# Attention and Fourier mixing on one core: slots in twos, an earlier copy of the mask's factors, and work moved from TensorE and GpSimd to VectorE

## The chip, the cores and the metric

The kernel runs on one core of one Trainium2 chip. The metric is the time of one execution in microseconds (us) on the device. Executions of one kernel lie within 0.1 to 0.7% of each other here. A difference of 2% is the threshold for calling a change faster or slower.

## The reference

Four batches of block-sparse attention (8 heads, 768 positions, head size 64) are joined into x of 768 x 512. Each x then goes through a Fourier mixing with a normalised two-layer channel product.

```python
scores = scale * np.matmul(q, k.transpose(0, 1, 3, 2))      # (4, 8, 768, 768)
scores = np.where(mask, scores, -1e9)                       # window, global and random blocks of 32
attn = np.exp(scores - max); attn = attn / attn.sum(-1)
x = np.matmul(attn, v)                                      # joined to (4, 768, 512)
u = x + np.real(np.fft.fft2(x))                             # along seq and d_model
un = (u - mean(u)) / np.sqrt(var(u) + 1e-6)
out = u + np.maximum(un @ w_ch1, 0.0) @ w_ch2
```

## The kernel before

The heads go in 16 pairs, four pairs per batch. A pair's weights are made in 12 units of 128 keys by 384 queries, and two units are one **slot**, so there are 96 slots, 24 per batch. From the second batch on, the mixing of the batch before (folds on VectorE, Fourier products `zp` on TensorE, then channel products `xp`, `yp`, `z`, `y`) is put between the slots. The order of all instructions is fixed when the kernel is built: a small model of the engines (`when`, `busy`) decides what fits where.

A slot computes the scores s of its two units, then adds o of the two units of the slot before:

```python
def slot(sl):
    phase, r = divmod(sl, SB)          # SB = 24 slots per batch
    n, s = divmod(sl, SP)              # pair, slot of the pair
    units = range(SLOT * sl, SLOT * sl + SLOT)
    if sl < B * SB:
        for u, ps in scores(units):    # PE: s <- qT,kT, and s <- factors for the mask
            weigh(u, ps)               # ACT: exponential; then sums of the weights
    ...
    if 0 < sl <= B * SB:
        done = [u - SLOT for u in units]
        for u in done:
            values(u)                  # PE: o <- e,vr
    ...
    for at, a, half in ((1, 0, 0), (2 if n > 0 else 3, 0, 1), (4, 1, 0), (5, 1, 1)):
        if s == at and n + 1 < BY_VECTOR:                       # BY_VECTOR = 2 * NP + 1 = 9
            short.append(("t", 0.0, lambda a=a, half=half: turn(n + 1, a, half)))   # on PE
    ...
    if BY_VECTOR <= n + 1 < len(pairs):                         # on VectorE
        for at, fn, args in ((0, squares, (n + 1, 0)), (1, flip_blocks, (n + 1, 0)),
                             (2, in_order, (n + 1,)), (4, flip_blocks, (n + 1, 1)),
                             (5, squares, (n + 1, 1))): ...
    w_steps(sl)                        # VectorE rounds a chunk of the channel weights
    if sl == SB - 3:
        keep_factors()
```

Where TensorE adds the mask itself (the first batch, and the second until its channel products begin), it multiplies two small factors into the scores. These factors first lie in the two buffers that the second batch needs for its sums of weights, so they are copied away near the end of the first batch, into a buffer that a weight chunk used before:

```python
at_k = acc_p.tile([P, 2, 2 * HS], BF16, tag="acc", name="at_k")   # acc_p has two buffers
at_q = acc_p.tile([P, 2, 2 * HS], BF16, tag="acc", name="at_q")
factors = {"at": (of_k, off_q)}
def keep_factors():
    kept = room(2, [P, 2, S], "factors", BF16)
    for a, t in enumerate(factors["at"]):
        nc.sync.dma_start(out=kept[:, a, :], in_=t)
    factors["at"] = kept[:, 0, :], kept[:, 1, :]                   # used from the next slot on
```

From the second batch on, the sum of the weights over the keys is gathered by GpSimd, two adds of 384 columns per unit (`acc<-acc,e`), and `total` sums it over the partitions on TensorE (`sp<-acc,pick`).

## Time and profile before

| | before |
|---|---|
| time, median of the 4 runs beside the changed kernel | 1088.8 us (1086.9 to 1092.2) |
| span of the profiled run | 1090.0 us |
| start of slot 20, 24, 48, 72 (from the trace) | 104.5, 129.0, 296.1, 559.2 us |
| TensorE's waits, slots 20 to 24 / slot 24 to the end | 3.7 / 15.4 us |

"TensorE's waits" are all the holes between the end of one matmul record and the start of the next, added up over the trace. The span is divided at the starts of slots, because a slot is the same piece of the attention in every version; how much of the mixing lies ahead of it can differ. From the page of the kernel before, the shares of the chain that ended last, and the group of GpSimd's adds (line, engine, operation, output and inputs, shape, count; then busy us and mean ns; then the idle time ahead and what ended it):

```profile
PE 88%; DVE 6%; ACT 2%; issue 1%; DMA 1%; SPq 1%; POOL 0%; DVEq 0%; ACTq 0%; POOLq 0%
...
L602 POOL TENSOR_TENSOR acc<-acc,e 128x384 f32<-128x384 f32 x192 | 200.4, 1077 | 128.4 <-DVE e L590 118.8
```

The chain is TensorE's for 88%, and VectorE, ScalarE and transfers come in only where TensorE waits. GpSimd's 200 us of adds are on the chain for 0%, so moving some of them away can help only by what waits behind them.

### The profile page before, as it was taken

The page shows a single profiled execution, that of the slowest core. Times are in us where ns is not written, and L with a number is a line of the kernel's source. Part 1 is how long each engine was busy: PE and PEld are TensorE (multiplying, and loading weights), DVE is VectorE, ACT ScalarE, POOL GpSimd, SP SyncE. Part 2 cuts the span into 40 slices and gives each one's busy share as a digit, 9 for nine tenths or more (in the row PEclk, how much of TensorE's full clock was granted, in tenths as well). Part 3 has the DMA queues.
Part 4 walks back from the last instruction along what each step waited for, and adds up shares of the span by engine and source line. Part 5 has one row for each costly group of instructions (what it writes and reads, how often), then busy time and mean ns, then how long its engine had stood idle before and what let it go on. Part 6 is the DMA issues. An engine that isn't in the chain of part 4 may idle for free.

```text
span 1090.0 us, 12509 instructions
## 1 busy us (share of the span) xinstructions
PE 1056.0 (97%) x4410; PEld 538.6 (49%) x4410; DVE 648.6 (60%) x1203; ACT 378.8 (35%) x762; POOL 274.2 (25%) x302
## 2 busy tenths in 40 slices
PE   8999879999999999999999999999999999999996
PEld 4333335454444555443444555443344555568575
DVE  5899682664468255665577446555556355575663
ACT  5988644552331212343342302334230202220210
POOL 1000084852243001355455000344630001000000
PEclk9999899999999999999999999999999999999998
DMA  7757311110010001223211000212000001000001
GB/s 223 229 164 240 94 30 30 39 35 15 15 29 1 1 0 31 57 39 55 44 21 32 1 0 15 63 33 39 13 8 7 1 0 30 29 1 0 1 19 44
DMA packets 108483, 47.07 MB, mean 43 GB/s; under 512 B 95854, under 2 KB 101244, under 8 KB 108412
## 3 DMA queue, kind: packets, MB, share of 16 engines
q1 hardware_dynamic: 106524, 45.38, 16.4%
q10 hardware_dynamic: 1856, 0.79, 0.3%
q8 instruction: 37, 0.61, 0.2%
q14 instruction: 34, 0.28, 0.1%
q0 software_dynamic: 32, 0.01, 0.0%
HBM read 37.11 MB, written 6.29 MB: 40 GB/s over the span
## 4 chain that ended last, share of the span: by engine, by line
PE 88%; DVE 6%; ACT 2%; issue 1%; DMA 1%; SPq 1%; POOL 0%; DVEq 0%; ACTq 0%; POOLq 0%
PE y L1066 23%; PE z L1010 15%; PE s L565 11%; PE o L615 10%; PE yp L1010 8%; PE yy L1129 6%; PE xp L1010 4%; PE zp L823 2%; PE tp L498 1%; PE sp L681 1%; PE s L575 1%; PE utp L935 1%; PE zp L794 1%; SPq L653 1%; PE sp L695 1%
## 5 line engine op out<-in xcount | busy, mean ns | idle before, releaser
L602 POOL TENSOR_TENSOR acc<-acc,e 128x384 f32<-128x384 f32 x192 | 200.4, 1077 | 128.4 <-DVE e L590 118.8
L565 PE MATMUL s<-qT,kT 64*128 64x384 f32 x768 | 154.4, 517 | 5.3 <-DVE e L590 3.8
L615 PE MATMUL o<-e,vr 128*64 128x384 f32 x768 | 148.7, 509 | 0.0
L1069 DVE TENSOR_TENSOR x<-y,x 128x512 f32<-128x512 f32 x72 | 49.7, 691 | 147.8 <-PE y L1066 147.8
L1066 PE MATMUL y<-w_sb,hA 128*128 128x512 f32 x288 | 131.1, 598 | 1.7 <-ACT zs L825 1.7
L1066 PE MATMUL y<-w_sb,hB 128*128 128x512 f32 x288 | 129.0, 597 | 0.7 <-DVE x L1069 0.7
L590 DVE TENSOR_TENSOR e<-s,mask 128x768 f32<-128x768 f32 x106 | 96.3, 949 | 46.6 <-ACT s L588 44.9
L588 ACT ACTIVATE s<-s 128x768 f32<-128x768 f32 x106 | 80.3, 789 | 118.2 <-PE s L565 117.6
L602 POOL TENSOR_TENSOR acc<-e 128x384 f32<-128x384 f32 x48 | 49.9, 1061 | 237.6 <-ACT e L585 129.1
L565 PEld LDWEIGHTS s<-qT,kT 64*128 64x128 f32 x768 | 63.7, 186 | 80.4 <-issue 23.0
L1010 PE MATMUL z<-unT,t 128*128 128x384 f32 x256 | 93.0, 486 | 0.0
L1015 DVE TENSOR_TENSOR hA<-z,hA 128x384 f32<-128x384 f32 x64 | 35.7, 558 | 89.5 <-PE z L1010 88.7
L1066 PEld LDWEIGHTS y<-w_sb,hB 128*128 128x128 f32 x288 | 53.2, 190 | 67.6 <-issue 65.8
L615 PEld LDWEIGHTS o<-e,vr 128*64 128x64 f32 x768 | 47.4, 138 | 76.3 <-issue 72.3
L1066 PEld LDWEIGHTS y<-w_sb,hA 128*128 128x128 f32 x288 | 52.4, 190 | 65.7 <-issue 58.5
L886 POOL TENSOR_SCALAR st<-st 128x1 f32<-128x1 f32 x24 | 6.7, 280 | 280.6 <-DVE st L885 280.2
L585 ACT ACTIVATE e<-s 128x768 f32<-128x768 f32 x86 | 65.0, 812 | 28.0 <-PE s L575 26.6
L1019 ACT ACTIVATE hA<-hA 128x384 f32<-128x384 f32 x64 | 33.5, 523 | 117.8 <-DVE hA L1015 117.4
L1010 PEld LDWEIGHTS z<-unT,t 128*128 128x128 f32 x256 | 48.6, 190 | 33.9
L1019 ACT ACTIVATE hB<-hB 128x384 f32<-128x384 f32 x64 | 33.5, 523 | 86.5 <-DVE hB L1015 86.5
L1010 PE MATMUL xp<-unT,w_sb 128*128 128x384 f32 x128 | 47.7, 495 | 0.3 <-DVE x L1069 0.3
L1010 PE MATMUL yp<-unT,w_sb 128*128 128x384 f32 x128 | 46.9, 489 | 0.5 <-DVE un L859 0.5
(202 smaller groups left out, 1389.7 us busy)
## 6 DMA issues: line engine op xcount, KB each, us to landing
wraw<-in_moe_w_ch_dram SPq DMA_DIRECT2D x32, 512.0 KB
vr<-in_v_dram SPq DMA_DIRECT2D x30, 192.0 KB
qr<-in_q_dram SPq DMA_DIRECT2D x48, 64.0 KB
x<-oT SPq DMA_DIRECT2D x192, 12.0 KB
kr<-in_k_dram SPq DMA_DIRECT2D x14, 192.0 KB
qb<-in_q_dram SPq DMA_DIRECT2D x28, 96.0 KB
kb<-in_k_dram SPq DMA_DIRECT2D x28, 96.0 KB
out_dram<-x SPq DMA_DIRECT2D x16, 128.0 KB
```

What stands on the lines that cost most here:

```text
L565: nc.tensor.matmul(s[:, i, 0:HS], kT[rows, c * P:(c + 1) * P], qT[rows, queries], start=True, stop=u not in by_pe)
L585: nc.scalar.activation(out=e, in_=s[:, :, 0:HS], func=ACT.Exp, scale=scale)
L588: nc.scalar.activation(out=s[:, :, 0:HS], in_=s[:, :, 0:HS], func=ACT.Exp, scale=scale)
L590: nc.vector.tensor_tensor(out=e, in0=s[:, :, 0:HS], in1=m.broadcast_to([P, 2, HS]), op=ALU.mult)
L602: nc.gpsimd.tensor_add(out=acc, in0=e_of[u - 1][:, i, :] if c == 1 else acc, in1=e[:, i, :])
L615: nc.tensor.matmul(o[D * i:D * i + D, :], vt[:, i, c, :], e[:, i, :], start=(c == 0), stop=(c == C - 1))
L1010: nc.tensor.matmul(to, a[:, k, :], c[:, k, :], start=(k == 0), stop=(k == ND // 2 - 1))
L1015: tt(out=to, in0=ps, in1=a, op=ALU.add)
L1019: nc.scalar.activation(out=h, in_=h, func=ACT.Relu)
L1066: nc.tensor.matmul(y, hs[0, half][:, l, m * P:(m + 1) * P], w2_sb[:, 4 * r + l, :], start=(l == 0), stop=(l == 3))
L1069: nc.vector.tensor_tensor(out=x[:, m, :], in0=y, in1=x[:, m, :], op=ALU.add)
L1129: nc.tensor.matmul(ps, a[:, k, :], c[k // 2][:, k % 2, :] if isinstance(c, list) else c[:, k, :], start=(k == 0), stop=(k == 3))
```

## The change

In the main the change does five things. It runs slots in twos from the first channel products on, about 250 us into the run (s, o, o, s in place of s, o, s, o), so that TensorE changes its tiling mode less often. It gives VectorE some of the second batch's adds (one of 768 columns in place of two of 384). It turns q and k of pairs 5 to 8 on VectorE. It puts measured durations into the model. And it copies the mask's factors two slots earlier. (It also moves the start of the mixing, some loads and one bank of transposes, in lines not shown.) Its core, with cuts:

```diff
-    BY_VECTOR = 2 * NP + 1
+    BY_VECTOR = NP + 1
 ...
+    def gather(u):
+        ...
+        if u in by_pe and factors["at"] and max(when["DVE"], at) + 1.0 < max(when["POOL"], at) + 2.9:
+            nc.vector.tensor_tensor(out=acc, in0=start, in1=e, op=ALU.add)
+            acc_at[n, half] = busy("DVE", 1.0, at) + HOP
+        else:
+            for i in range(2):
+                nc.gpsimd.tensor_add(out=acc[:, i, :], in0=start[:, i, :], in1=e[:, i, :])
+            acc_at[n, half] = busy("POOL", 2.9, at) + HOP
 ...
+        OPS = {fold_0: 1, fold_1: 1, fold_e: 3, fold_2: 2}     # folds: longer beside GpSimd
 ...
+        opens = sl % 2 == 0
+        state["paired"] |= opens and len(late) > 0
+        paired = state["paired"]
 ...
+        if paired and len(due) == 2 and due[0] % SP % T == T - 1:
+            sum_up()
+        got = scores(units) if sl < B * SB else ()
+        if paired and len(due) == 2:
+            sum_up()
+        for u, ps in got:
+            weigh(u, ps)
 ...
-        if sl == SB - 3:
+        if sl == SB - 5:
             keep_factors()
```

More of the change, by code (lines that the diff above doesn't have):

```diff
@@ L481, with turn_on @@
     turned, e_of, acc_of, o_of, sums_of, x_of, sp_of = {}, {}, {}, {}, {}, {}, {}
-    s_at, e_at, oT_at, acc_at = {}, {}, {}, {}
+    s_at, e_at, e_free, oT_at, acc_at = {}, {}, {}, {}, {}
+    def turn_on(n, a, half):
+        return "m" if n > NP and (a, half) == (0, 1) else "t"
     def turn(n, a, half):
         t = loaded[n, a]
-        if half == 0:
+        first_of = (n, a) not in turned
+        if first_of:
             turned[n, a] = tp_p.tile([P, S], FP32, tag="qk"[a] + "T", name="qk"[a] + "T")
@@ L490, in turn @@
         first = n == 0 and half == 0
-        tag, pool = ("m", ps_m) if first and a == 0 else ("t", ps_t)
+        tag, pool = ("m", ps_m) if first and a == 0 or turn_on(n, a, half) == "m" else ("t", ps_t)
         tp, at = pool.tile([P, 512], FP32, tag=tag, name="tp"), bank(tag)
@@ L510, in turn @@
             give(at, end)
-        if half == 1:
+        if not first_of:
             flat = t.rearrange("p t r i d -> p (t r i d)" if a == 0 else "p c i d -> p (c i d)")
@@ L585, in weigh @@
             nc.scalar.activation(out=e, in_=s[:, :, 0:HS], func=ACT.Exp, scale=scale)
-            e_at[u] = busy("ACT", 0.8, s_at[u]) + HOP
+            e_at[u] = busy("ACT", 0.8, max(s_at[u], e_free.pop(u - 2 * SLOT, 0.0))) + HOP
         else:
@@ L592, in weigh @@
             e_at[u] = busy("DVE", 0.97, busy("ACT", 0.8, s_at[u]) + HOP) + HOP
-        if n < NP:
+            if n >= NP:
+                gather(u)
+    def gather(u):
+        n, w = divmod(u, UP)
+        half, c = divmod(w, C)
+        if c == 0:
             return
-        if c > 0:
-            acc_at[n, half] = busy("POOL", 2.0, e_at[u]) + HOP
         if c == 1:
             acc_of[n, half] = acc_p.tile([P, 2, HS], FP32, tag="acc", name="acc")
-        for i in range(2 if c > 0 else 0):
-            acc = acc_of[n, half][:, i, :]
-            nc.gpsimd.tensor_add(out=acc, in0=e_of[u - 1][:, i, :] if c == 1 else acc,
-                                 in1=e[:, i, :])
+        acc, e = acc_of[n, half], e_of[u]
+        start = e_of[u - 1] if c == 1 else acc
+        at = max(e_at[u], acc_at.get((n, half), 0.0))
+        if u in by_pe and factors["at"] and max(when["DVE"], at) + 1.0 < max(when["POOL"], at) + 2.9:
[5 more added lines that the diff above has]
+            acc_at[n, half] = busy("POOL", 2.9, at) + HOP
+        e_free[u] = acc_at[n, half]
     def values(u):
@@ L616, in values @@
                              start=(c == 0), stop=(c == C - 1))
+        if u in by_pe and n >= NP:
+            gather(u)
         if c == C - 1:
@@ L901, in d @@
         def d(us, fn, *args):
-            return "d", lambda: fn(*args), 0.0, 0.0, us
+            return "d" + "d" * OPS.get(fn, 0), lambda: fn(*args), 0.0, 0.0, us
+        OPS = {fold_0: 1, fold_1: 1, fold_e: 3, fold_2: 2}
         first = [d(1.8, fold_0, 0), d(1.8, fold_0, 1), d(1.0, fold_1, 0), d(0.9, fold_e),
@@ L1207, with behind @@
     W_PACE = 1.42
-    short, apart, late = deque(), deque(), deque()
-    state = {"w": 0, "got": 0, "owed": 0.0, "ready": 0.0}
+    short, apart, late, due = deque(), deque(), deque(), deque()
+    asked = set()
+    needed = set()
+    state = {"paired": False, "total": None, "w": 0, "got": 0, "owed": 0.0, "ready": 0.0}
     def channel_step():
         late.popleft()[0]()
+    def behind(kind):
+        at = max(when["DVE"], state["ready"])
+        return 0.75 * (len(kind) - 1) if when["POOL"] > at else 0.0
     def do_apart():
         kind, fn, pe, act, dve, _ = apart.popleft()
-        if kind in "dw":
+        if kind[0] in "dw":
+            dve += behind(kind)
             state["ready"] = busy("DVE", dve, rstd_at[0] if kind == "w" else state["ready"]) + HOP
@@ L1241, in gap @@
                 break
-            if kind in "dw":
+            if kind[0] in "dw":
+                dve += behind(kind)
                 if kind == "w" and rstd_at[0] > max(when["DVE"], when["PE"]) + 0.2:
@@ L1281, in begin, with rest, once @@
         apart.append(("-", go, 0.0, 0.0, 0.0, hold))
+    def rest():
+        return state["owed"] if late and state["owed"] >= late[0][1] / 2 else 0.0
+    def once(*of):
+        if of in asked:
+            return False
+        asked.add(of)
+        return True
     def w_loads():
@@ L1296, in slot, with sum_up @@
         units = range(SLOT * sl, SLOT * sl + SLOT)
-        if sl < B * SB:
-            for u, ps in scores(units):
-                weigh(u, ps)
-        if not late:
-            gap(1.5)
-        if 0 < sl <= B * SB:
-            done = [u - SLOT for u in units]
+        opens = sl % 2 == 0
+        state["paired"] |= opens and len(late) > 0
+        paired = state["paired"]
+        def sum_up():
+            at = due.popleft()
+            done = range(SLOT * at, SLOT * at + SLOT)
             for u in done:
                 values(u)
-            if phase == 0 or sl == SB:
+            if at < SB:
                 add_up(done)
@@ L1309, in slot @@
                 e_of.pop(u)
-        if s == 3 and n + 2 < len(pairs):
+        if paired and len(due) == 2 and due[0] % SP % T == T - 1:
[5 more added lines that the diff above has]
+            weigh(u, ps)
+        if not paired and not late:
+            gap(1.5)
+        while due and (opens or not paired):
+            sum_up()
+        due.append(sl)
+        if s >= (4 if paired else 3) and n + 2 < len(pairs) and (n + 2, 0) not in loaded:
             load_q(n + 2)
@@ L1315, in slot @@
         reuse = n % NP == 0 and phase >= 2
-        if sl > 0 and s == (5 if reuse else 3) and sl <= B * SB:
+        if s >= (5 if reuse else 3) and (n, 0) in oT_at and once(n):
             b, j = pairs[n]
@@ L1339, in slot @@
             short.append(("t", acc_at[n - 1, 1], lambda: total(n - 1)))
+            state["total"] = short[-1]
+        if r == 0:
+            needed.clear()
+            needed.update(map(id, short))
         if n + 1 < len(pairs):
-            for at, a, half in ((1, 0, 0), (2 if n > 0 else 3, 0, 1), (4, 1, 0), (5, 1, 1)):
-                if s == at and n + 1 < BY_VECTOR:
-                    short.append(("t", 0.0, lambda a=a, half=half: turn(n + 1, a, half)))
+            for at, a, half in ((1, 0, 0), (2 if n > 0 else 3, 0, 1),
+                                (3 if paired else 4, 1, 0), (5, 1, 1)):
+                if s >= at and n + 1 < BY_VECTOR and once(n + 1, a, half):
+                    short.append((turn_on(n + 1, a, half), 0.0,
+                                  lambda a=a, half=half: turn(n + 1, a, half)))
             if s == 1:
@@ L1351, in slot @@
             short.append(("m", 0.0, lambda: mask_step(sl - 4)))
-        if r == 1 and 0 < phase:
+        if r > 0 and 0 < phase and not needed.intersection(map(id, short)) and once("mixing", phase):
             begin(phase - 1)
@@ L1357, in slot @@
         state["owed"] = min(state["owed"], pace) + pace if late else 0.0
-        gap(max(state["owed"], 0.0))
-        while late and state["owed"] >= late[0][1] / 2:
+        more = paired and opens and sl < B * SB
+        if not more:
+            gap(rest())
+        while not more and rest():
             state["owed"] -= late[0][1]
             channel_step()
-            gap(max(state["owed"], 0.0))
-        while short and (s in (2, 5) or len(short) > 1 or phase == 0 or r == 0):
+            gap(rest())
+        must = (3, 5) if paired else (2, 5)
+        soon = r == 0 and all(i[1] < when["PE"] + 1.0 for i in short)
+        if s == 1 and state["total"] in short:
+            short.remove(state["total"])
+            state["total"][2]()
+        while short and (not more or soon) and (
+                s in must or len(short) > 1 or phase == 0 or soon or sl == B * SB):
             ready = [i for i in short if max(i[1], min(free[i[0]])) <= when["PE"] + 0.1]
-            if not ready and s not in (2, 5) and r > 0 and sl > 1:
+            if not ready and s not in must and 1 < sl < B * SB and not soon:
                 break
```

## The prediction

> **What bounds the kernel now.** I read the page's busy table and its slices first.
>
> ```profile
> PE 1056.0 (97%) x4410; PEld 538.6 (49%) x4410; DVE 648.6 (60%) x1203; ACT 378.8 (35%) x762; POOL 274.2 (25%) x302
> PE   8999879999999999999999999999999999999996
> POOL 1000084852243001355455000344630001000000
> PEclk9999899999999999999999999999999999999998
> ```
>
> TensorE is the bound: 97% busy, and a busy span can be lengthened only by more matmul time or a stall. So I ask two things: what matmul time the change takes away, and which stalls (the slices with 8 or less; the clock dips in slice 4, and in the windows of 25 us at 100 to 125 and 150 to 175, 0.86 each) it removes or makes. For the first I read TensorE's timeline, start to start, where the third batch's slots lie between channel products:
>
> ```profile
> 316.43 3.70 PE L1066 MATMUL y<-w_sb,hA 128*128 128x512 f32 x8
> 320.06 1.56 PE L565 MATMUL s<-qT,kT 64*128 64x384 f32 x8
> 321.55 1.51 PE L615 MATMUL o<-e,vr 128*64 128x384 f32 x8
> 322.99 3.70 PE L1066 MATMUL y<-w_sb,hA 128*128 128x512 f32 x8
> ```
>
> A slot is s (1.49 us) and o (1.44 us). Eight records of either cost 4 x 0.316 = 1.26 us in steady state (the starts of successive pairs inside a group lie 0.316 apart). The y group takes 3.63 us here, 3.44 us where another full-array group is on both sides. So each change between full array, two row tiles (s) and two column tiles (o) costs 0.15 to 0.2 us, three per slot: about 0.55 us.
>
> For the stalls I list TensorE's waits along the same timeline:
>
> ```profile
> 113.40 1.62 PE L565 MATMUL s<-qT,kT 64*128 64x384 f32 x8 [0.36 <-ACT e L585]
> 118.39 0.82 PE L575 MATMUL s<-factors 64*128 64x384 bf16 x4 [3.37 <-DMA factors<-at_q]
> 119.15 0.90 PE L637 MATMUL xt<-ident,oT 128*128 128x128 f32 x3
> 119.98 2.83 PE L615 MATMUL o<-e,vr 128*64 128x384 f32 x8
> ...
> 142.78 0.44 PE L498 MATMUL tp<-ident,qr 128*128 128x128 f32 x2 [1.12 <-ACT qT L507]
> ...
> 159.93 1.56 PE L794 MATMUL zp<-cs_sb,sa 128*128 128x385 f32 x4 [3.64 <-DVE sa L767]
> 162.19 1.01 PE L795 MATMUL zp<-cs_sb,e 128*128 128x192 f32 x2 [0.71 <-DVE e L767]
> ...
> 465.68 1.78 PE L565 MATMUL s<-qT,kT 64*128 64x384 f32 x8 [1.73 <-DVE e L590]
> ```
>
> After each long wait the same o group takes 2.83 us instead of 1.51 us: the clock has halved, and that costs another 2 to 3 us.
>
> **What the Trainium skill says.** "TensorEngine Tiling (Array Packing)", Key Properties: changing the tiling mode, not just the tile, drains TensorE. The 0.15 to 0.2 us per change agrees. "TensorE: Matmul & The Clock Gate", Part 1: after an idle window of about 3.4 us the clock falls to half until a busy window has passed. The waits of 3.37 and 3.64 us followed by double durations agree. "SBUF — State Buffer", Who interferes with whom: a VectorE instruction with two SBUF inputs and a GpSimd instruction that reads SBUF shut each other out for their whole length. Here the scaling of x (L723) takes 0.68 us alone and 1.48 us beside GpSimd's adds, which grow from 1.00 to 1.44 us: agrees.
>
> **The change, part by part.** I used the order of instructions of both programs; TensorE's, VectorE's and ScalarE's are the same up to the 20th slot (of 96).
>
> 1. *Transposes of q and k of pairs 5 to 8 go to VectorE.* 48 transposes fewer at 0.109 us: -5.2 us of TensorE. The two places where a pair's second q transpose waited for the one bank (1.12 us at 142.78 and 212.33) go too: -2.2 us. VectorE gets 4 x (0.96 + 1.52) us; ScalarE gets four reorderings of six copies, 2 x (0.43 + 0.31 + 0.19) = 1.9 us each.
> 2. *Slots in twos, s o o s instead of s o twice.* Going through both TensorE orders group by group, with each other tile shape counted as its own mode, I count 337 changes of mode before and 293 after: 44 x 0.19 = -8.4 us. Valuing every group by the shortest time that its kind took between the same neighbours gives the same sum for parts 1 to 3 within 2 us.
> 3. *The mask is added by TensorE for 4 slots longer in the second batch* (the mixing of the first batch is released later): 16 bf16 matmuls at 0.08 us and their mode changes, +1.7 us.
> 4. *VectorE adds up 23 of the second batch's units, 768 wide,* about 0.9 us each. GpSimd loses 46 adds of 1.0 to 1.5 us. Neither is TensorE's time, but GpSimd's adds were interleaved with the folds that the first Fourier product waits for (159.93). That product now also stands some two slots later. The wait (3.64 + 0.71) and the slow clock after it (about 3 us: o 2.83 for 1.51, the second zp group 2.20 for 1.4, the rest smaller) should go: -7.5 us.
> 5. *The copy of the mask's factors is issued in slot 19 instead of 21, and first used in slot 20 instead of 22.* This looks like a gain of 6 us. I do not believe it. The copy writes a buffer that the 27th weight chunk used, and in both programs it waits for the same VectorE instruction, that chunk's last rounding. The timelines of VectorE and of the DMA queue:
>
> ```profile
> 109.79 0.69 DVE L461 TENSOR_TENSOR w_sb<-w_sb,wraw 128x512 f32<-128x512 f32 x1
> ```
> ```profile
> 110.39 3.82 SPq L252 DMA_DIRECT2D qr<-in_q_dram  x6
> 114.31 0.55 SPq L478 DMA_DIRECT2D factors<-at_k  x1
> 114.91 0.60 SPq L478 DMA_DIRECT2D factors<-at_q  x1
> ```
>
> That rounding ends at 110.5. Before, the copy then stood behind six loads of q, went at 114.31 and released TensorE at 118.39, 4.1 us later. After, it can go at 110.5 and release at about 114 (3.3 to 4.1 us). But slot 20 wants it where it now does its mask matmuls, at 105.92. So TensorE waits about 8 us instead of 3.4, and pays the slow clock as before: +4.5 us.
>
> 6. *New waits in the second batch.* There a slot is now s 1.39, mask 0.42, o 1.44 = 3.26 us, with less else between. ScalarE needs 2 x 0.8 us for its exponentials, and their PSUM banks are wanted again about 2 us after the mask matmuls end. So some 0.5 us is left per slot; a reordering of 1.9 us or one that waits for a VectorE still folding uses it up. Four times about 1 us, plus squares and adds that hold the four weight buffers, plus the end of the stage, where VectorE has adds, a turn and the differences in a row: +6 us, an estimate, the least certain term.
> 7. *Batches three and four.* Runs of slots without channel work wait for weights (1.73 us at 465.68 and again at 720.17; 0.2 us in single slots). In twos, two o groups lie between some s groups, so part of this goes: -3 us.
>
> Sum: -5.2 - 2.2 - 8.4 + 1.7 - 7.5 + 4.5 + 6 - 3 = -14.1 us. 1087.5 - 14.1 = 1073.4, so **1073 us**, 1.3% less. The end (after the last attention slot TensorE's order is the same) contributes nothing.
>
> **Rivals.**
> - *The factor copy is in time.* For: it no longer stands behind the q loads, and that is plainly why it was moved. Against: the rounding's end at 110.5. If it were in time, parts 5 and the old loss change from +4.5 to -6: about 1063 us, faster by over 2%.
> - *VectorE becomes the bound of the second batch.* It is busy 59 of the 102 us from 129 to 231; adds (21 us) and turns (10 us) are added to a stage that also gets shorter. For: 90 us of work in some 95 us, in strict order, with TensorE's weights waiting on adds behind folds. Against: part of today's 59 us is waiting for GpSimd, which shrinks, and the last part of the stage's work is the channel stage's. If it binds, +10 us more: about 1083.
> - *The mode changes are hidden or the pairs starve on PSUM.* Between s and the next s there must be exponential and mask product of two units, about 2.7 us; the doubled o gives 2.7 us, a single o at a half's end only 1.44. If each of some 24 pairs waited 0.3 us, 7 us of part 2 is given back: about 1080.
>
> **Range and chances.** The certain part (1, 2, 3) is about -14 us; the stalls (4 to 7) are near zero in sum, each several us uncertain. All favourable gives 1060, all unfavourable 1085. 8 in 10: 1061 to 1084. Faster by 2% means below 1065.7, which needs the factor copy in time or nearly no new waits: 0.22. Slower by 2% would take a new bound through three batches: 0.01.
>
> **What would show it right or wrong.** Part 5: a wait of about 8 us at the first matmul with factors, near 114 us, DMA named, and slow groups after it; right if over 6, wrong if under 2. Part 4: no wait over 1 us at the first zp group. Part 2: o in groups of 16 records at about 2.7 us, s of the second slot without a wait. Part 1: no tp group after 130 us. Part 6: waits of s for ScalarE's e between 130 and 230, in sum 4 to 8 us. TensorE's busy time should fall by 10 to 14 us, plus or minus what the slow clock changes. The prediction is wrong if TensorE's stalls, counted from its timeline, do not come to about the 22 us of today less some 5.

## The result, and the profile after

The changed kernel is correct. Its median is **1080.86 us** (1080.1 to 1081.2, 4 runs), that of the kernel before 1088.81 us beside it. Ratios in this text are the mean time of one kernel's runs over that of the other's of the same rounds, so not quite the ratio of the medians. Here it is 0.9923, with a 95% interval of 0.9895 to 0.9950: about 0.8% less, within 2%.

The page of the changed kernel, where the prediction showed that of before (busy time, then TensorE's slices in tenths of busy time, then GpSimd's):

```profile
PE 1042.1 (97%) x4378; PEld 537.1 (50%) x4378; DVE 661.5 (61%) x1226; ACT 376.4 (35%) x742; POOL 227.4 (21%) x256
...
PE   8999789999999999999999999999999999999996
POOL 1000062323600001265454000354630001000000
```

TensorE's busy time fell by 13.9 us, but the span only by 10.5 (1090.0 to 1079.5). The fifth slice is worse, 7 for 8. TensorE's timeline there (start, length, engine, line, operation, and in brackets the idle time ahead of it and its releaser), with the last instruction of the weight chunk on VectorE and the copy in the DMA queue:

```profile
104.92 1.56 PE L570 MATMUL s<-qT,kT 64*128 64x384 f32 x8
115.64 0.82 PE L580 MATMUL s<-factors 64*128 64x384 bf16 x4 [9.16 <-DMA factors<-at_q]
116.39 2.83 PE L633 MATMUL o<-e,vr 128*64 128x384 f32 x8
```
```profile
110.17 0.69 DVE L462 TENSOR_TENSOR w_sb<-w_sb,wraw 128x512 f32<-128x512 f32 x1
```
```profile
110.92 0.53 SPq L479 DMA_DIRECT2D factors<-at_k  x1
111.50 0.60 SPq L479 DMA_DIRECT2D factors<-at_q  x1
```

TensorE arrives at slot 20's mask product at 106.5 and stands for 9.16 us: the copy goes out at 110.92, just after the rounding ends at 110.86, and releases TensorE at 115.64. The o group after it takes 2.83 us where others take 1.51: the trace grants TensorE half its clock from 110.92 to 121.16.

The first Fourier product, which had waited 3.64 us, waits no more. Eleven microseconds ahead of it there is a new wait. TensorE's timeline, then VectorE's:

```profile
162.35 2.93 PE L570 MATMUL s<-qT,kT 64*128 64x384 f32 x8 [4.53 <-DVE kT L537]
...
173.02 1.56 PE L814 MATMUL zp<-cs_sb,sa 128*128 128x385 f32 x4
```
```profile
152.42 1.76 DVE L614 TENSOR_TENSOR acc<-acc,e 128x768 f32<-128x768 f32 x1
154.10 2.54 DVE L766 TENSOR_TENSOR sa<-x 128x1536 f32<-128x1536 f32 x1
156.57 2.55 DVE L766 TENSOR_TENSOR sd<-x 128x1536 f32<-128x1536 f32 x1
159.05 1.74 DVE L770 TENSOR_TENSOR sa<-sa 128x765 f32<-128x765 f32 x1
160.71 1.49 DVE L537 STREAM_TRANSPOSE kT<-kb 128x768 f32<-128x768 f32 x1
```

Pair 5's scores need k turned. That turn stands in VectorE's queue behind one add and three folds, and starts at 160.71, when TensorE has been idle for 2.9 us.

The ledger by stretches of the program, in us:

| stretch | before | after | difference | TensorE's waits before / after |
|---|---|---|---|---|
| start to slot 20 | 104.5 | 104.9 | +0.4 | 2.9 / 2.9 |
| slot 20 to 24 | 24.5 | 30.3 | +5.8 | 3.7 / 9.5 |
| slot 24 to TensorE's end | 951.5 | 934.8 | -16.7 | 15.4 / 12.9 |

### The profile page after: what moved, and what is told of

Its sections match the earlier page's. It is cut to its first block, busy times and chain, and to the rows that moved or that the text cites.

```text
span 1079.5 us, 12378 instructions
## 1 busy us (share of the span) xinstructions
PE 1042.1 (97%) x4378; PEld 537.1 (50%) x4378; DVE 661.5 (61%) x1226; ACT 376.4 (35%) x742; POOL 227.4 (21%) x256
## 4 chain that ended last, share of the span: by engine, by line
PE 90%; DVE 6%; issue 2%; ACT 1%; DMA 0%; POOL 0%; SPq 0%; ACTq 0%; POOLq 0%; DVEq 0%
PE y L1089 23%; PE z L1033 15%; PE s L570 12%; PE o L633 11%; PE yp L1033 8%; PE yy L1152 6%; PE xp L1033 4%; PE zp L843 2%; PE sp L701 1%; PE s L580 1%; PE zp L814 1%; PE tp L503 1%; PE utp L958 1%; PE sp L715 1%; PE xt L657 1%
## 5 line engine op out<-in xcount | busy, mean ns | idle before, releaser
L619 POOL TENSOR_TENSOR acc<-acc,e 128x384 f32<-128x384 f32 x154 | 156.8, 1055 | 212.2 <-ACT e L590 137.6
L633 PE MATMUL o<-e,vr 128*64 128x384 f32 x768 | 142.8, 500 | 0.0
L595 DVE TENSOR_TENSOR e<-s,mask 128x768 f32<-128x768 f32 x98 | 89.0, 950 | 54.2 <-ACT s L593 48.5
L593 ACT ACTIVATE s<-s 128x768 f32<-128x768 f32 x98 | 74.3, 791 | 84.2 <-PE s L570 83.9
L590 ACT ACTIVATE e<-s 128x768 f32<-128x768 f32 x94 | 71.2, 812 | 42.6 <-PE s L580 38.6
L619 POOL TENSOR_TENSOR acc<-e 128x384 f32<-128x384 f32 x40 | 42.9, 1094 | 111.9 <-PE sp L715 85.7
L1053 ACT COPY hA<-xp 128x384 f32<-128x384 f32 x32 | 15.3, 479 | 113.0 <-PE xp L1033 113.0
```

The source lines that it names most:

```text
L590: nc.scalar.activation(out=e, in_=s[:, :, 0:HS], func=ACT.Exp, scale=scale)
L593: nc.scalar.activation(out=s[:, :, 0:HS], in_=s[:, :, 0:HS], func=ACT.Exp, scale=scale)
L595: nc.vector.tensor_tensor(out=e, in0=s[:, :, 0:HS], in1=m.broadcast_to([P, 2, HS]), op=ALU.mult)
L619: nc.gpsimd.tensor_add(out=acc[:, i, :], in0=start[:, i, :], in1=e[:, i, :])
L633: nc.tensor.matmul(o[D * i:D * i + D, :], vt[:, i, c, :], e[:, i, :], start=(c == 0), stop=(c == C - 1))
```

## The experiments

The open questions were what the copy costs by itself, whether the new wait for k is one of order or of amount on VectorE, what the turn and the twos are worth, and why a busy time 14 us lower gives only 8 us. All twelve runs gave correct results. They ran in three calls of four, with 11 runs of the kernel before beside each call, so kernels of different calls are compared by their ratios to it.

| run | median us | ratio to before (95%) |
|---|---|---|
| changed kernel | 1080.86 | 0.9923 (0.9895 to 0.9950) |
| e1 late first use of the copy | 1069.05 | 0.9822 (0.9797 to 0.9848) |
| e2 k turned a slot earlier | 1081.74 | 0.9940 (0.9917 to 0.9963) |
| e3 both | 1069.77 | 0.9828 (0.9803 to 0.9853) |
| e8 copy as before | 1074.89 | 0.9882 (0.9859 to 0.9906) |
| e4 turn on TensorE | 1083.26 | 0.9944 (0.9925 to 0.9963) |
| e6 no twos | 1105.39 | 1.0151 (1.0128 to 1.0175) |
| e7 before, late first use | 1083.15 | 0.9951 (0.9924 to 0.9979) |
| e9 short lead | 1075.79 | 0.9879 (0.9857 to 0.9901) |
| e10 e1, short lead of folds | 1065.75 | 0.9785 (0.9761 to 0.9809) |
| e11 twos in the fourth batch only | 1085.11 | 0.9965 (0.9942 to 0.9987) |
| e12 e1, more adds on GpSimd | 1071.66 | 0.9836 (0.9811 to 0.9861) |
| e13 e10 with a shorter lead | 1068.32 | 0.9808 (0.9784 to 0.9833) |

Against the line of 2%, e1, e10 and e13 are unclear, for their intervals hold 0.98; all others are within 2%.

### e1: the copy as in the change, first read in slot 24

```diff
-        factors["at"] = kept[:, 0, :], kept[:, 1, :]
+        factors["kept"] = kept[:, 0, :], kept[:, 1, :]
 ...
+        if sl == SB - 1:
+            factors["at"] = factors["kept"]
```

> The changed kernel with one edit: the copy of the mask's factors is issued where the change issues it, but is first read in slot 24, not in slot 20; until then VectorE multiplies the mask in. Theory A (the early use of the copy costs a TensorE wait of 9.2 us and about 2.5 us of slow clock after it): the wait at the first matmul with factors is under 0.3 us, slots 20 to 24 take 20 to 22 us and not 30.3, and the time is 10 to 13 us under the changed kernel's 1080.9, about 1069. Rival B (VectorE and the folds are what binds there, TensorE's wait only lets them catch up): the wait goes, but waits for VectorE of the same size appear between 125 and 165 us, and the time falls by less than 6 us, to 1075 or more.

The expectation misnames one thing: until slot 24 it is TensorE that adds the mask, from the original factors, not VectorE. That makes the test cleaner, as the same matmuls read another address. TensorE's timeline at slot 24:

```profile
123.46 1.56 PE L570 MATMUL s<-qT,kT 64*128 64x384 f32 x8
124.85 0.49 PE L580 MATMUL s<-factors 64*128 64x384 bf16 x4
```

There is no wait. Slots 20 to 24 take 18.5 us in place of 30.3, everything after slot 24 is as long as in the changed kernel (935.5 against 934.8), and the time falls to 1069.05 us. Theory A holds, and the stretch is even shorter than the 20 to 22 us that it named: the early use of the copy cost the changed kernel 11.8 us by the medians (11.0 by the ratios), and nothing was given back.

### e8: the copy in slot 21 again, as before the change

```diff
-        if sl == SB - 5:
+        if sl == SB - 3:
```

> The changed kernel with the copy of the factors issued in slot 21 again, as before the change, and first read in slot 22. Theory A (the copy can't go before VectorE's rounding of the 27th weight chunk ends at 110.9 us, so only the place of first use matters): the wait at the first matmul with factors is 1 to 4 us and not 9.2, about what the kernel before had (3.4), and the time is 5 to 8 us under the changed kernel, 1073 to 1076. Rival B (the early issue did bring the copy forward in the queue, and the late issue puts it behind the loads of q again by about as much): the wait is 6 us or more and the time is within 3 us of the changed kernel.

The DMA queue and TensorE of e8:

```profile
110.90 2.89 SPq L223 DMA_DIRECT2D qb<-in_q_dram  x4
113.89 0.53 SPq L479 DMA_DIRECT2D factors<-at_k  x1
```
```profile
118.10 0.50 PE L580 MATMUL s<-factors 64*128 64x384 bf16 x4 [2.58 <-DMA factors<-at_q]
```

The copy does go 3 us later, behind the loads of q, and releases TensorE at 118.10 in place of 115.64. But TensorE now asks for it at 115.5 and not at 106.5, so the wait is 2.58 us and the time 6.0 us under the changed kernel's (4.5 by the ratios). Theory A again: putting the copy forward by two slots bought 2.5 us of release and took 9 us of slack.

### e7: the kernel before with the late first use

```diff
-        factors["at"] = kept[:, 0, :], kept[:, 1, :]
+        factors["kept"] = kept[:, 0, :], kept[:, 1, :]
 ...
+        if sl == SB - 1:
+            factors["at"] = factors["kept"]
```

> The kernel before with one edit: the copy of the factors is issued as before, in slot 21, but first read in slot 24. Theory A (the first use of the copy costs the kernel before its wait of 3.4 us and about 2.5 us of slow clock as well, and nothing else needs that time): 5 to 7 us under the kernel before, ratio 0.993 to 0.996. Rival B (the wait only let VectorE catch up, and the wait of 3.6 us at the first Fourier product grows by as much): within 2 us of the kernel before.

The ratio is 0.9951, some 5 us. Slots 20 to 24 take 18.4 us in place of 24.5, and the wait at the first Fourier product stays at 3.64 us. So the kernel before lost about 6 us at the same place, and the change made it 12. Without this step on either side, the rest of the change is worth some 14 us (1083.15 to 1069.05, and the same by the two ratios).

### e2 and e3: k turned one slot earlier, alone and with e1

```diff
-                                 (2, in_order, (n + 1,)), (4, flip_blocks, (n + 1, 1)),
+                                 (2, in_order, (n + 1,)), (3 if n < 2 * NP else 4, flip_blocks, (n + 1, 1)),
```

> The changed kernel with one edit: for pairs 5 to 8 VectorE turns k one slot earlier (slot 3 of the pair before, not slot 4). Theory A (the wait of 4.5 us at 162 us for pair 5's k, and some 1.7 us of slow clock after it, come only from where the turn stands in VectorE's queue behind the folds): the wait is gone or under 1 us and the time is 4 to 6 us under the changed kernel, 1075 to 1077. Rival B (VectorE is short of time in this stage): the folds and the first Fourier product, or the next exponentials, wait instead, and the time falls by less than 2 us. The 9.2 us wait for the factors stays in both.

> Both edits of the two runs beside it: factors first read in slot 24, k turned one slot earlier. If the two waits are independent, the gains add: about 12 + 5 us under the changed kernel, 1063 to 1065, and faster than the kernel before by over 2%. If VectorE has no spare time in the second batch, the gain is that of the better of the two edits alone, 1069 or more.

Theory A missed. e2 is 1081.74 us, e3 1069.77: no gain over the kernel that each rests on, as Rival B and the second case of e3 said, though what waits is none of the things that Rival B named. TensorE's timeline of e2, then VectorE's:

```profile
168.01 1.49 PE L715 MATMUL sp<-acc,pick 128*32 128x384 f32 x4 [3.86 <-DVE acc L614]
```
```profile
166.79 0.29 DVE L788 TENSOR_TENSOR e<-e 128x128 f32<-128x128 f32 x1
167.00 0.95 DVE L614 TENSOR_TENSOR acc<-acc,e 128x768 f32<-128x768 f32 x1
```

The wait for k is gone. But the last add of pair 4's second half stands behind the same folds, ends at 167.95, and the sum of the weights waits 3.86 us for it. The wait moved to the next instruction that TensorE wants from that queue. The Trainium skill's page "Perfetto Trace Analysis", Tensor Engine Instruction, says that VectorE's queue is strictly first in, first out; the timelines agree: the add starts at 167.00, right behind the fold ahead of it, when TensorE has stood for 2.9 us. The result leaves open whether the queue has too much work or a bad order.

### e9: a shorter lead for VectorE's folds

```diff
-    ALONE = 3.0          # how far VectorE may end behind TensorE's place, no channel work there
+    ALONE = 1.5
```
on top of e1.

> The kernel of the late first use (e1, 1069.05 us) with one more edit: while no channel product is there, a fold may be put into VectorE's queue only if it is to end at most 1.5 us after TensorE's place, not 3.0; so pair 5's k turn and the adds come between the folds and not behind them. Theory A (VectorE has the time in this stage, the wait of 4.5 us is one of order in its queue): the wait at pair 5's first scores falls under 1.5 us without another of over 2 us taking its place, and the time is 4 to 7 us under e1, 1062 to 1065. Rival B (VectorE's amount of work up to the first Fourier product binds): the wait moves to that product or to the sum of the weights, 3 us or more, and the time is within 2 us of e1.

It missed in the other direction: 1075.79 us, 6.7 us over e1. The stretch in question did gain, as from slot 24 to 36 it takes 57.3 us against e1's 61.0. The constant also governs the end of that stage. TensorE of e9 there:

```profile
248.16 1.56 PE L1033 MATMUL z<-t,w_sb 128*128 128x384 f32 x4 [1.99 <-DVE e L595]
...
254.15 2.54 PE L1033 MATMUL z<-unT,t 128*128 128x384 f32 x4 [2.53 <-DVE hA L1038]
```

In e1 no wait there is over 0.8 us. The constant touched more than the disputed folds, so the run is no verdict on them.

### e10 and e13: the shorter lead for the second batch's folds alone

```diff
+    FOLDS = 1.5          # e13: 0.5
 ...
-                if max(when["DVE"], state["ready"]) + dve > when["PE"] + rest + ahead:
+                lead = min(ahead, FOLDS) if len(kind) > 1 and not late else ahead
+                if max(when["DVE"], state["ready"]) + dve > when["PE"] + rest + lead:
```
on top of e1.

> The kernel of the late first use (e1, 1069.05 us) with the shorter lead of e9 (1.5 us) for the folds of the second batch alone, so that the instructions after them stand as in e1; pair 5's k turn moves ahead of the second fold, and one add ahead of a fold. e9 was 3.6 us ahead of e1 at the 36th slot and lost it again after the 44th. Theory A (what e9 lost came from the other instructions whose lead it shortened): the gain of the 36th slot, 2 to 4 us, stays to the end, 1065 to 1067. Rival B (the add that still stands behind the folds makes the sum of the weights wait, as in e3): the wait of 4.5 us only moves there, and the time is within 1.5 us of e1.

> As e10 with a lead of 0.5 us in place of 1.5: now two adds and the sum's copy as well stand ahead of the last folds, which is e9's order of VectorE in that stretch, and the rest as in e1. Theory A (order in VectorE's queue, not its amount of work, made the wait): no wait over 2 us between 140 and 170 us, 3.5 to 5.5 us under e1, 1063.5 to 1065.5, and faster than e10. Rival B (the first Fourier product now waits for the folds that come later): a wait of 2 us or more at that product, and within 1.5 us of e1.

e10 is the best kernel, **1065.75 us**, ratio 0.9785 (0.9761 to 0.9809). By the traces, two things differ from e1 in VectorE's queue: k's turn stands ahead of the second fold, and one add more stands ahead of a later one. The expectation calls that add moved; it came over from GpSimd (VectorE 24 adds in place of 23, GpSimd 192 in place of 194). VectorE, then TensorE of e10:

```profile
141.90 2.54 DVE L766 TENSOR_TENSOR sa<-x 128x1536 f32<-128x1536 f32 x1
144.37 1.53 DVE L537 STREAM_TRANSPOSE kT<-kb 128x768 f32<-128x768 f32 x1
```
```profile
146.05 1.56 PE L570 MATMUL s<-qT,kT 64*128 64x384 f32 x8 [0.43 <-DVE kT L537]
...
151.10 0.92 PE L570 MATMUL s<-qT,kT 64*128 64x384 f32 x4 [0.88 <-ACT e L590]
...
155.02 0.84 PE L715 MATMUL sp<-acc,pick 128*32 128x384 f32 x4 [0.47 <-DVE acc L614]
```

Three waits of 1.8 us in sum stand where one of 4.5 us stood, and no group runs at half clock after them (in e1 the granted clock is 0.5 from 148.40 to 155.22). Slots 24 to 48 take 116.2 us against e1's 120.1, all later stretches agree within 0.1 us. VectorE's busy time is not lower (662.5 us; 661.7 in e1). So k's wait was one of order, and e13 shows it without the add: there the turn has the same place, each engine has as many adds as in e1, and k waits 0.43 us again. The whole gain need not be order alone. GpSimd stood still from 145.3 to 150.3 in e10, and the second fold took 1.72 us in place of 2.56, the next 0.92 in place of 1.74. What the shorter folds and the add from GpSimd gave was not tested apart.

e13 went too far. TensorE of e13:

```profile
154.44 0.84 PE L715 MATMUL sp<-acc,pick 128*32 128x384 f32 x4 [2.06 <-DVE acc L614]
...
158.78 0.55 PE L657 MATMUL xt<-ident,oT 128*128 128x128 f32 x3 [2.07 <-DVE sums L683]
```

k is in time as in e10, but the sum of the weights waits 2.06 us for an add, and the next transpose another 2.07 us for VectorE's copy of that sum, which stands behind four folds. Slots 24 to 48 take 120.8 us, and the gain is gone. This is the outcome of Rival B at another place: the Fourier product had no wait, the instructions ahead of it had.

### e12: more of the adds on GpSimd

```diff
-        if u in by_pe and factors["at"] and max(when["DVE"], at) + 1.0 < ...
+        if u in by_pe and factors["at"] and max(when["DVE"], at) + 1.8 + 1.0 < ...
```
on top of e1.

> e1 (1069.05 us) with 17 adds of 768 on VectorE in the second batch in place of 23, and 12 more of 384 on GpSimd; two of the six stood ahead of the folds that pair 5's k turn waits behind. Theory A (VectorE's backlog at that turn is the sum of what stands ahead of it, two adds of 1 to 1.75 us among it): the wait of 4.5 us falls to 2 to 3 us and the time is 1 to 3 us under e1. Rival B (GpSimd's adds alternate with VectorE's folds, so that work handed back to GpSimd lengthens each fold by about as much): the wait and the time stay within 1 us of e1, or grow.

Rival B, and rather more: k's wait grew from 4.54 to 5.56 us and the time by 2.6 us (1.5 by the ratios). VectorE's scaling of x (six instructions) in e1 and then in e12:

```profile
135.29 5.39 DVE L743 TENSOR_TENSOR x<-x,r 128x512 f32<-128x512 f32 x6
140.60 1.75 DVE L614 TENSOR_TENSOR acc<-acc,e 128x768 f32<-128x768 f32 x1
```
```profile
134.77 7.88 DVE L743 TENSOR_TENSOR x<-x,r 128x512 f32<-128x512 f32 x6
```

In e12 the add is not in VectorE's queue, but the scaling ran beside GpSimd's adds for longer and took 7.88 us, as against 5.39 + 1.75. The work given back to GpSimd cost VectorE at least as much as the add itself. A version with all adds on GpSimd could not be run, because the order of its instructions deadlocks; so what the adds on VectorE are worth in all stays open.

### e4: q and k of pairs 5 to 8 turned by TensorE again

```diff
-    BY_VECTOR = NP + 1
+    BY_VECTOR = 2 * NP + 1
```

> The changed kernel with one part undone: q and k of pairs 5 to 8 are turned by TensorE again. Theory A (what the turn on VectorE saves, 48 transposes at 0.109 us or 5.2 us, it loses again in the wait of 4.5 us for pair 5's k and the slow clock after it): TensorE's busy time rises by about 4 us, the wait near 162 us is gone, and the time is within 2.5 us of the changed kernel's 1080.9. Rival B (the wait belongs to VectorE's folds and adds in this stage and comes back at another operand, as it did when k was turned one slot earlier): a wait of 3 us or more stays between 140 and 180 us and the time is 4 to 7 us over the changed kernel. The 9.2 us wait for the factors stays in both, or is a little shorter, for the transposes fill some of it.

The median is 2.4 us over the changed kernel's. TensorE's busy time is 1046.9 us, 4.8 more, and its waits from slot 24 to 48 are 1.9 us, 3.0 less, with none over 1 us. So Theory A holds: of what the turn on VectorE saves, the wait for k took back all but some 2 us. The edit is not quite the turn alone: the model then gave GpSimd four of VectorE's adds (19 in place of 23) and TensorE the mask products of two slots fewer, and q's second half keeps the other bank that the changed kernel gives it, so the two waits of 1.12 us of the kernel before are absent. No run has the turn on TensorE together with the late first use; with the 3 to 4 us of e10 over e1 added, the turn would be worth some 6 us without its wait, an estimate.

### e6 and e11: without twos, and with twos in the fourth batch only

```diff
-        state["paired"] |= opens and len(late) > 0
+        state["paired"] |= False                           # e6
 ...
-        paired = state["paired"]
+        paired = state["paired"] and phase != 2            # e11
```

> The changed kernel with one part undone: no slots in twos. Theory A (each change of tiling mode costs 0.15 to 0.2 us; this kernel has 26 more of them than the changed one by the order of its instructions, and the two waits of 1.7 us of the kernel before in runs of slots without channel work come back): 26 x 0.19 + 3.5 = 8.4 us slower, 1087 to 1091. Rival B (the twos gain little, for what they save in mode changes they lose in waits for PSUM banks and exponentials): within 3 us of the changed kernel. The first 250 us should hardly differ, for the slots in twos begin late in the second batch.

> The changed kernel with slots in twos in the fourth batch only, one by one in the third. It has 10 more changes of tiling mode than the changed kernel by the order of its instructions. Theory A (mode changes at 0.19 us, and one wait of 1.7 us in a run of slots without channel work in the third batch, are what twos save there; e6's 13 us of waits near 710 to 750 us belong to single slots in the fourth batch): 2 to 4.5 us slower than the changed kernel's 1080.9, 1083 to 1085.5, and no wait over 2 us after 650 us. Rival B (those 13 us come from channel work that the third batch without twos left for later): waits of several us appear after 690 us again, and the time is 12 us or more over the changed kernel.

e6 is slower than either expectation, 1105.39 us or 24.5 us over the changed kernel. The first 254 us are the same. The trace has 13 us more of waits after slot 48, led by one in the fourth batch. TensorE, then ScalarE:

```profile
710.93 2.93 PE L570 MATMUL s<-qT,kT 64*128 64x384 f32 x8 [8.80 <-DVE e L595]
```
```profile
706.94 0.48 ACT L658 COPY x<-xt 128x384 f32<-128x384 f32 x1 [8.84 <-DMA out_dram<-x]
```

ScalarE's copy of the new x waits for the output of the batch two back to leave the same buffer; behind it in ScalarE's queue stand the exponentials, and behind them the scores. In e11, with single slots in the third batch and twos in the fourth, no such wait is there (the largest after 650 us is 1.8 us, at 698.64, which the changed kernel has too), and the time is 4.3 us over the changed kernel's, which is Theory A. From slot 48 to 95, e11 takes 2.65 us more, 0.64 of it waits; the remaining 2.0 us over 10 more changes of mode is 0.20 us each, an estimate that gives all of it to them. So e6's 24.5 us is not the price of its 28 more changes. Most of it comes from single slots in the fourth batch: 13 us of waits, and a granted clock of 0.5 in three stretches after 704 us (17 us). Why single slots there bring the copy ahead of the output was not tested and stays open.

## Why the prediction was right or wrong

The range (1061 to 1084) held and "within 2%" was the likeliest class. The point, 1073, was 7.9 us too low. Of these, 1.3 us is the base (1087.5 when the prediction was made, 1088.8 beside the changed kernel) and 0.4 the rounding of 1073.4. The prediction's sum was -14.1 us; the two profiled runs differ by 10.5 us, the medians by 8. The profiled run of before took 1091.7 us, 2.9 over its kernel's median, while that of after is 0.3 over its own, so 2.6 us of the miss lies in the spread of the kernel before. That spread goes with the clock: of its 33 runs beside the experiments, those with a mean granted clock of 0.995 or more took 1085.2 to 1087.3 us, those with 0.989 or less (the profiled run has 0.989) 1090.3 to 1092.8. A cost of slow clock read from one trace is therefore that of one execution. The other 3.6 us can be found in the traces (the start, to slot 20, is +0.4; the rows below add +1.0, +0.1, +1.3, +0.5 and +0.3 to the prediction):

| part | predicted | measured | |
|---|---|---|---|
| 1 to 3, without waits | -11.9 | -10.9, as what is left of the 10.5 by the other rows | near; 0.20 us per change of mode by e11, 0.19 assumed, but fewer changes |
| 1, 4: waits for the one bank and at the first Fourier product | -9.7 | -6.6: those waits are 0; about -3.0: their slow clock went too | right |
| 5: the factor copy, slots 20 to 24 | +4.5 | +5.8 | right, undersized |
| 6: new waits in the second batch | +6 | +4.9 of waits and about 1.6 of slow clock | size near by luck, cause wrong |
| 7: batches three and four | -3 | -0.8 of waits (after slot 48: 8.8 to 8.0) and about -1.9 of slow clock | size near by luck |

- **Parts 1 to 3** counted 44 changes of mode fewer. The traces show 38 (381 before, 343 after, counting each change of a matmul's tile shape from one record to the next). At 0.19 us that makes the term -10.7, close to what is left.
- **Part 5** is the step that decided, and it was read from the profile before: the rounding's end binds the copy, not the queue. The wait was 9.16 us and not about 8, because the copy took 4.7 us from issue to release, where 3.3 to 4.1 was assumed. e1, e7 and e8 show it three ways. The rival "in time" is refuted.
- **Part 6** expected four waits of about 1 us for ScalarE's exponentials. There is one of 4.53 us, for VectorE's turn of k, so the test "in sum 4 to 8 us" was met by another wait. The prediction named a VectorE "still folding" as a risk for the reordering of q, but did not set pair 5's k against the folds in VectorE's order. That is the view that was missing: both orders could be listed, and the turn stood right behind three folds of 2.5, 2.5 and 1.7 us.
- **Part 7** was to come from shorter waits, and those fell by 0.8 us only: the two of 1.73 us did go, but 1.82 us at a channel product (696.65) and two of about 0.8 us came in. What brought it near -3 is a slow clock that the prediction had not counted: in the profiled run of before the granted clock is 0.5 from 721.14 to 724.56, after the wait at 720.17, and two groups there take 1.9 us longer. After, no such stretch follows.
- **The rival "VectorE becomes the bound"** is half right. VectorE held TensorE up, but e10 has the same VectorE busy time and 1.8 us of waits there. The rival that pairs starve on PSUM is refuted: a double o takes 2.7 us as assumed, and e11 is slower without twos.
- The last test in the prediction, that TensorE's waits should come to 22 less some 5, did not follow from its own terms: 22 - 2.2 - 4.35 + 4.6 + 6 - 3 = 23. They came to 25.3, so that test failed.

## What to carry to other kernels

Moving a transfer's issue forward helps only if what it waits for is done by then; its first reader should not move with it. Here the latest slot at which the original had to be given up was the right one. Where in-order engines share a stage, list what the bound engine needs from each queue and what stands ahead of it: a wait that moves when its instruction is moved is a matter of order for the whole queue, and k's turn in a better place, with one add taken over from GpSimd, was worth 3 to 4 us. When an adder competes with folds for VectorE, look at both before moving work back to GpSimd.

## What the Trainium skill lacked or had wrong

- "TensorEngine Tiling (Array Packing)", Key Properties, says that a change of mode drains TensorE but gives no cost. e11 has 10 more changes and 2.0 us more outside waits: 0.20 us each, an estimate.
- "TensorE: Matmul & The Clock Gate", Part 1, gives one idle window of about 3.4 us as what halves the clock, and tells of one kernel in which frequent short idles did it, without their length. Shorter waits were followed by half clock here. The granted clock is 0.5 from 160.19 to 163.60 in e13, after waits of 2.06 and 2.07 us with 2.3 us of work between (the first Fourier group took 2.23 us, start to start, in place of 1.40); from 254.58 to 258.00 in e9, after 1.99 and 2.53 us (a z group took 2.33 us in place of 1.29); and from 721.14 to 724.56 in the kernel before, after a single wait of 1.73 us. But it stays at 1 after 2.58 us in e8 and after the other wait of 1.73 us in the kernel before (465.68), so the length of a wait alone does not decide it. The prediction saw agreement because it looked at the waits of 3.37 and 3.64 us only.
- "SBUF — State Buffer", Who interferes with whom, has VectorE operations with two inputs and GpSimd's reads shut each other out, but not how much a row of such operations is stretched by adds on GpSimd. Here six scalings of x took 5.39 us in e1 and 7.88 us in e12, where GpSimd had more adds beside them.
